# Attention, Fourier and feed-forward in one kernel: instruction order from a model clock instead of written-out counts

## The chip, the core and the metric

The kernel runs on one core of a Trainium2 chip. The metric is the device time of one execution, in microseconds. The median of three runs before the change is 1101.29 us (1101.19 to 1104.8). Engines: TensorE (PE in the rows; PEld are its weight loads), VectorE (DVE), ScalarE (ACT), GpSimd (POOL) and SyncE (SP), on whose queue all DMAs are issued. Each engine works through its own queue in order, and an instruction that waits for a semaphore holds up all that stand behind it on that engine.

## The reference

Three parts follow one another, for 4 batches of 448 rows and 768 features (12 heads of 64):

```python
scores = scale * np.matmul(q, k.transpose(0, 1, 3, 2)) - np.log(S)
attn = 1.0 / (1.0 + np.exp(-scores))
x = np.matmul(attn, v)                       # then heads side by side: (4, 448, 768)

mixed = np.real(np.fft.fft(np.fft.fft(x, axis=1), axis=2))
u = x + mixed
un = (u - mu) / np.sqrt(var + 1e-06)         # over the 768 features
y = u + np.maximum(un @ w_ch1, 0.0) @ w_ch2  # 768 -> 3072 -> 768

gate = sigmoid(causal convolution of y over 5 rows, per feature)
out = (gate * (y @ w_val)) @ w_out
```

The weights come in as float64. The kernel turns them into float32 by integer operations on VectorE, takes a power of two from the largest absolute value, and splits each matrix into a high and a low float16 half. Activations are split the same way, and three products (high x high, high x low, low x high) give the result.

## The kernel before

Features lie in six blocks of 128 partitions, rows along the free axis; `acc` holds one batch (six blocks x 448) from attention to the end.

*Attention* runs 84 steps: 24 pairs of heads (6 a batch), 7 steps for two pairs. A step is four score matmuls into `ps_s` (two buffers, L360), a sigmoid on ScalarE (L367) and, a step later, four value matmuls into `ps_m` (L380). At the end of a pair ScalarE copies one half of the result to `acc` (L386) and VectorE adds the other (L389). `ps_m` has four banks for everything else.

*Fourier* of a batch (`fourier`): the batch is folded into sums and differences of feature blocks (L399, L423) and of rows (L417 to L427), scaled by a power of two from the largest |v| (L112 to L168), split into halves `ph`, `pl` (L439), transformed over features by 40 matmuls (L468, L472), split again into `zh`, `zl` on the way out of PSUM (L268, L459), mixed over rows by 48 matmuls (L487), and added to `acc` (L494, L497). Some rows go over a small extra table (`eo`, `sp`, `e16`), which is filled by DMA.

*Norm* (`norm`): sums over the feature blocks (L569), a mean matmul (L575), centring (L588), squares (ScalarE), their sums (L591, L593), a variance matmul (L603), `rs` (L605, L606), a spread matmul (L619), scaling (L632) and halves (L626).

*Feed-forward*: 8 groups of 384 hidden features x 4 batches. `up` has 54 matmuls (L737), ScalarE and VectorE split its result (L744, L746); `down` has 54 (L760), added to `acc` by VectorE (L764). The blocks go up 0, up 1, down 0, down 1, up 2, down 2, up 3, and then up n+1, down n. A group's weights are brought in by `load_group`: chunks by DMA (L179), absolute value (L187 or L190), maximum (L198), conversion (L200, L203, L206), high half (L236, L237) and low half (L239, on GpSimd; L242, on VectorE, for the first group).

*Value and projection*, 24 blocks of 18 matmuls each (L939, L964), end the kernel.

What sets the order: the code is written out in one go, and what goes beside the main matmuls is a set of Python generators that are advanced by counts. In attention each step advances the Fourier (`fq`), the norm (`lq`) and the weights (`wq`) by fixed numbers; `ROOM`, `FOLD_AT`, `W_RATE`, `PACE`, `FFN_RATE`, `bank()` and the bare loops of `yield` in `fourier` and `norm` are such counts. Folds and sums go to GpSimd or VectorE by batch number (`E = P if b < 3 else V`). Loads of q, k and v are issued at two fixed places of each seven steps. The first weight group is loaded during attention, in chunks of 256 columns with two buffers; later groups have chunks of 384.

## Time and profile before

| | |
|---|---|
| median of the runs | 1101.29 us |
| the profiled execution | 1104.88 us |
| its span, first to last instruction | 1103.0 us |
| TensorE busy | 1042.5 us |
| VectorE busy | 709.3 us |
| ScalarE busy | 422.3 us |
| GpSimd busy | 178.6 us |
| mean granted TensorE clock | 0.981 |

The slices of the page show where it is lower. A matmul's busy time depends on the granted clock too, so a stretch can be busy all the time and yet slow; PEclk tells this. The launch lies in the 1.9 us between span and execution.

### The profile page before, as it was taken

How to read it: one execution, taken by the hardware profiler on the slowest of the kernel's cores; microseconds unless marked ns; L12 is line 12 of the kernel's file. 1: busy time of each engine (PE TensorE's matmuls, PEld its weight loads, DVE VectorE, ACT ScalarE, POOL GpSimd, SP SyncE). 2: the span in 40 equal slices, each digit the busy share in tenths (PEclk: the TensorE clock that was granted, in tenths of full speed). 3: DMA queues.
4: the chain of work that ended last, by engine and by line, in shares of the span. 5: the costliest groups of instructions: out<-in, count | busy, mean ns of one | idle time of the engine just before them, and what ended most of it. 6: DMA issues, size and time to landing. Idle time of an engine off the chain costs nothing.

```text
span 1103.0 us, 15620 instructions
## 1 busy us (share of the span) xinstructions
PE 1042.5 (95%) x6116; PEld 534.4 (48%) x6116; DVE 709.3 (64%) x1580; ACT 422.3 (38%) x630; POOL 178.6 (16%) x157
## 2 busy tenths in 40 slices
PE   9789688998979999999999999999999999999998
PEld 4244243455544455545555555555555545555554
DVE  2755678687966565776556676665666768777530
ACT  5455544544124333323333332233333274443321
POOL 0103323230002111111111101111110152000000
PEclk9899988999999999999999999999999999999999
DMA  7522223111111222333122333122233200001001
GB/s 228 171 79 83 89 67 112 33 31 30 30 29 47 68 72 72 86 86 86 43 60 73 84 86 86 48 69 71 72 86 86 59 1 1 1 26 42 34 34 67
DMA packets 34921, 72.57 MB, mean 66 GB/s; under 512 B 3956, under 2 KB 16672, under 8 KB 34848
## 3 DMA queue, kind: packets, MB, share of 16 engines
q1 hardware_dynamic: 34848, 71.58, 22.6%
q8 instruction: 48, 0.79, 0.3%
q14 instruction: 25, 0.20, 0.1%
HBM read 65.88 MB, written 5.51 MB: 65 GB/s over the span
## 4 chain that ended last, share of the span: by engine, by line
PE 73%; DVE 16%; DMA 4%; ACT 4%; issue 2%; POOL 2%; SPq 0%; ACTq 0%; DVEq 0%
PE ps_m L760 25%; PE ps_s L737 24%; PE ps_m L939 7%; PE ps_m L964 7%; PE ps_m L380 3%; DMA w<-w1d 2%; PE ps_s L360 2%; PE ps_m L468 2%; DVE acc L764 1%; PE ps_m L487 1%; DMA w<-w2d 1%; DVE wf L206 1%; DVE un L588 1%; DVE wabs L198 1%; DVE wf L203 1%
## 5 line engine op out<-in xcount | busy, mean ns | idle before, releaser
L737 PE MATMUL ps_s<-un,w1hi 128*128 128x448 f16 x1152 | 313.8, 354 | 4.9 <-DVE un L626 3.3
L760 PE MATMUL ps_m<-hh,w2hi 128*128 128x448 f16 x576 | 204.4, 355 | 5.5 <-DVE acc L764 4.1
L760 PE MATMUL ps_m<-hl,w2hi 128*128 128x448 f16 x576 | 204.2, 354 | 1.1 <-DVE hl L746 1.1
L760 PE MATMUL ps_m<-hh,w2lo 128*128 128x448 f16 x576 | 204.2, 354 | 0.0
L737 PE MATMUL ps_s<-un,w1lo 128*128 128x448 f16 x576 | 203.9, 354 | 0.0
L760 PEld LDWEIGHTS <-w2hi 128*128 128x128 f16 x1152 | 112.9, 99 | 111.0 <-issue 8.6
L737 PEld LDWEIGHTS <-w1hi 128*128 128x128 f16 x1152 | 112.9, 98 | 107.8 <-issue 4.1
L764 DVE SCALAR_TENSOR_TENSOR acc<-ps_m,rg,acc 128x448 f32<-128x448 f32 x192 | 128.5, 678 | 29.0 <-PE ps_m L760 28.7
L187 ACT ACTIVATE wabs<-w 128x384 f32<-128x384 f32 (+1 forms) x109 | 58.4, 547 | 222.4 <-DMA w<-w2d 84.1
L198 DVE TENSOR_SCALAR_CACHE_REDUCE wabs<-wabs 128x384 f32<-128x384 f32 (+1 forms) x126 | 66.8, 530 | 55.1 <-ACT wabs L187 54.3
L746 DVE SCALAR_TENSOR_TENSOR hl<-ps_s,hh 128x896 f16<-128x896 f32 x64 | 54.6, 853 | 72.0 <-ACT hh L744 72.0
L360 PE MATMUL ps_s<-q,k 64*64 64x448 f32 x672 | 84.4, 568 | 14.0 <-ACT sg L367 13.5
L367 ACT ACTIVATE sg<-ps_s,logb 128x896 f32<-128x896 f32 x84 | 82.4, 1005 | 36.6 <-PE ps_s L360 36.5
L380 PE MATMUL ps_m<-sg,v 64*64 64x448 f32 x672 | 85.5, 568 | 3.1 <-DVE vg L130 1.7
L737 PEld LDWEIGHTS <-w1lo 128*128 128x128 f16 x576 | 56.5, 98 | 56.6 <-issue 4.4
L760 PEld LDWEIGHTS <-w2lo 128*128 128x128 f16 x576 | 56.7, 98 | 54.6 <-issue 2.7
L939 PE MATMUL ps_m<-xs,wvhi 128*128 128x448 f16 x288 | 78.0, 352 | 0.0
L200 DVE TENSOR_SCALAR wf<-wabs 128x384 int32<-128x384 int32 (+1 forms) x126 | 45.1, 358 | 50.1 <-POOL w1lo L239 19.1
L744 ACT ACTIVATE hh<-ps_s 128x896 f16<-128x896 f32 x64 | 46.1, 720 | 80.0 <-PE ps_s L737 80.0
L206 DVE SCALAR_TENSOR_TENSOR wf<-w,wf 128x384 int32<-128x384 int32 (+1 forms) x126 | 71.0, 563 | 2.9
L203 DVE SCALAR_TENSOR_TENSOR wf<-w,wf 128x384 int32<-128x384 int32 (+1 forms) x126 | 68.7, 545 | 2.5
L817 DVE SCALAR_TENSOR_TENSOR gp<-acc,cw,gp 128x448 f32<-128x448 f32 x72 | 49.3, 685 | 20.3 <-ACT gp L815 18.4
(174 smaller groups left out, 1230.7 us busy)
## 6 DMA issues: line engine op xcount, KB each, us to landing
w<-w1d SPq DMA_DIRECT2D x42, 384.0 KB
w<-w2d SPq DMA_DIRECT2D x42, 384.0 KB
q<-qd SPq DMA_DIRECT2D x24, 224.0 KB
out<-o SPq DMA_DIRECT2D x24, 224.0 KB
k<-kd SPq DMA_DIRECT2D x23, 224.0 KB
w<-wvd SPq DMA_DIRECT2D x12, 384.0 KB
w<-wod SPq DMA_DIRECT2D x12, 384.0 KB
v<-vd SPq DMA_DIRECT2D x12, 256.0 KB
```

What stands on the lines that cost most here:

```text
L187: A.activation(out=wa, in_=z[:, :, 1].bitcast(F32), func=AF.Abs)
L198: V.tensor_scalar(out=a, in0=a, scalar1=LEAST, scalar2=None, op0=ALU.max, op1=ALU.max, accum_out=m[:, i:i + 1])
L203: V.scalar_tensor_tensor(out=f.bitcast(I32), in0=lo, scalar=29, in1=f.bitcast(I32), op0=ALU.logical_shift_right, op1=ALU.bitwise_or)
L206: V.scalar_tensor_tensor(out=f.bitcast(I32), in0=hi, scalar=-0x40000000, in1=f.bitcast(I32), op0=ALU.bitwise_and, op1=ALU.bitwise_or)
L360: nc.tensor.matmul(p[HALVES[c], h, :S], k[HALVES[h], ks], q[HALVES[h]], start=True, stop=True)
L367: A.activation(out=sg, in_=sc.pop(t)[:, :, :S], func=AF.Sigmoid, scale=1.0 / math.sqrt(D), bias=logb)
L380: nc.tensor.matmul(xps[at, r][HALVES[h], :S], v[HALVES[r], s, HALVES[h]], a[HALVES[r], h], start=first, stop=last)
L737: nc.tensor.matmul(p[:, i, :S], w[:, k, fs], u[:, k], start=(m == 0), stop=(m == 17))
L760: nc.tensor.matmul(p[:, :S], w[:, f, js], hh[f // 2][k][:, f % 2], start=(m == 0), stop=(m == 3 * FC - 1))
L764: V.scalar_tensor_tensor(out=acc[b][:, j, PAD:], in0=p[:, :S], scalar=rg, in1=acc[b][:, j, PAD:], op0=ALU.mult, op1=ALU.add)
L939: nc.tensor.matmul(p[:, :S], w[:, k, js], u[:, k], start=(n == 0), stop=(n == 17))
L964: nc.tensor.matmul(p[:, :S], w[:, k, js], gs[b, k][i], start=(n == 0), stop=(n == 17))
```

## The change

A model clock (`Clock`) is kept while the code is written out. Every instruction passes through `Timed`, which adds a fixed cost for its form to the model time of its engine, after the model times of its operands and free buffers. The generators no longer count steps. They yield what they need next: `on(engines, operands, cost)` or `when(condition)`. A `Board` holds them with ranks; `pump` takes the one that is ready by the model, the lowest rank first, and writes its instruction down. Where a job names two engines (folds, sums, low halves of the norm, absolute values), it goes to the one that is done first by the model. `force` writes jobs down in order of their model time until a condition holds; the main code calls it where it can't go on without (weights of a group there, a PSUM bank free).

The clock exists only while the program is written; on the chip the engines still wait for semaphores alone.

With it come: weight chunks of 384 columns in attention too, three buffers for them (two before), their absolute values on ScalarE or VectorE by the model; loads of q, k and v up to seven steps ahead; one instruction for two feature blocks in the adds after mixing and in the norm; `ps_m` as four named banks, each taken until it is read; the second Fourier batch's start bound to the first one's end; the pools for the next weight group opened when the first group is done; a smaller scratch for dynamic DMAs. Matmuls are the same in number and form.

```diff
@@ -39,49 +40,343 @@
 HALF_AT = (1, 3, 5, 6)
 AHEAD = 7
 LAG = 1
-FOLD_AT = (14, 18)
-ROOM = {1: 4, 3: 4, 5: 4}
 WARM = 9
-W_RATE = (1.85, 0.5, 1.5)
-FFN_RATE = (0.5, 2.2, 2, 1.6)
-PACE = 3
+COLS = 384
+SOON = 1.3
+IDLE = 0.6
+STEP = 1.5
+EASE = 0.9
+FOLD_BY = "DVE", "POOL"
+SUM_BY = "DVE", "POOL"
+LOW_BY = "DVE", "POOL"
+W_AT = 0
+FIRST = 7
+TABLE = 8
+ABS_BY = "ACT", "DVE"
+W_RANK = 3.5
 ABSMAX = bass.bass_isa.ReduceOp.absmax
 LEAST = 2.0 ** (896 // 8 - 127)
 
...
+    def put(self, e, cost, reads, writes, lag=0.06, shared=False, tag=None):
+        need = max([self.ready(e, *reads)] + [self.free(e, a) for a in writes])
+        start = max(self.at[e], need)
+        if shared and start < self.port[0] and self.port[1] != e:
+            cost += 0.8 * min(cost, self.port[0] - start)
+        end = start + cost
+        if shared:
+            self.port = (end, e)
...
+    def best(self, act):
+        now = self.clock.at["PE"]
+        pick = None
+        for job in self.jobs:
+            if job[3] is None:
+                if job[4] < self.turn:
+                    return job, None
+                continue
+            engines, aps, cost, go = job[3]
+            if go is not None and not go():
+                continue
+            if not engines:
+                return job, None
+            for e in engines:
+                at = self.clock.at[e]
+                t = max(at, self.clock.ready(e, *aps))
+                wait = t - max(at, now)
+                if e == "PE":
+                    ok = t <= now + 0.05
+                elif e == "ACT":
+                    ok = t + cost <= act and (wait <= 0.1 or t <= now + 0.3)
+                else:
+                    ok = t <= now + (SOON if job[0] < 4 else IDLE) and (wait <= 0.1 or t <= now + 0.3)
+                if ok:
+                    key = wait > 0.1, job[0], job[1], t + cost * (1.1 if e == "POOL" else 1)
+                    if pick is None or key < pick[0]:
+                        pick = key, job, e
+        return pick and pick[1:]
...
-    def to_f32(pl, src, dst, n, m=None):
...
+        def fetch():
+            for k in range(num):
+                yield on("SP", go=lambda: gone[0] > k - 3)
+                w = pl.tile([128, step], I64, tag="w64", bufs=3, name="w64")
+                Q.dma_start(out=w, in_=src[:, k * step:(k + 1) * step])
+                got.append(w.bitcast(I32).rearrange("p (n t) -> p n t", t=2))
+
+        def absolute():
+            for k in range(num):
+                yield when(lambda: len(got) > k and gone[0] > k - 2)
+                wa = pl.tile([128, step], F32, tag="wabs", bufs=2, name="wabs")
+                e = yield on(ABS_BY, got[k], cost=0.55)
+                if e == "ACT":
+                    A.activation(out=wa, in_=got[k][:, :, 1].bitcast(F32), func=AF.Abs)
+                else:
+                    V.tensor_scalar(out=wa.bitcast(I32), in0=got[k][:, :, 1], scalar1=0x7FFFFFFF, scalar2=None, op0=ALU.bitwise_and)
+                ready.append(wa)
+
+        board.add(rank, fetch())
...
-    def fold_part(b, t):
-        x = acc[b][:, :, PAD:]
-        if t == 0:
-            folds[b] = [fk.tile([128, 3, 4 * NE], F32, tag="pm", bufs=2, name="pm") for _ in range(2)]
-        E = P if b < 3 else V
-        for pm, op in zip(folds[b], (ALU.add, ALU.subtract)):
-            E.tensor_tensor(out=pm[:, t, :S], in0=x[:, t], in1=x[:, t + 3], op=op)
...
+                yield when(lambda: b * NT + t + 3 in stored)
+                for pm, op in zip(q, OPS):
+                    e = yield on(FOLD_BY, x[:, t], x[:, t + 3])
+                    ENG[e].tensor_tensor(out=pm[:, t, :S], in0=x[:, t], in1=x[:, t + 3], op=op)
             for k in range(2):
...
+            for o in range(2):
+                yield when(lambda: len(hls) > o)
+                yield on("PE", *hls[o], e16, go=banks(2))
+                for c in range(2):
+                    if c:
+                        yield on("PE", go=banks(1))
+                    yield from dstep(o, c, hls[o])
+            stepped.add(b)
...
-    mixed, cst, credit = {}, [], [0.0]
+    sigmoid(0)
     for t in range(NSTEP):
-        i, at = t // 7 * 2, t % 7
-        b, r = divmod(t, PER)
-        pieces[0] = ROOM.get(at, 0)
+        at_step[0] = t
+        if t == W_AT:
+            board.add(W_RANK, first_weights())
         if t + 1 < NSTEP:
             scores(t + 1)
-        sigmoid(t)
-        if t == 0:
-            amax_v(0, 0)
-        if r == 16:
-            peak_v(b, 0)
-        if r == 17:
-            pieces[0] -= 2
...
-        drain(2)
+            board.pump(ck.at["PE"] + 0.12 + EASE)
+            sigmoid(t + 1)
+        board.pump(ck.at["PE"] + STEP + EASE)
...
+    def pump():
+        tend()
+        board.pump(ck.at["PE"] + SOON + 0.8)
+
+    def force(done):
+        board.force(lambda: tend() or done())
...
@@ -733,36 +1028,33 @@
                 m = 0
                 fs = slice((f + i) * 128, (f + i + 1) * 128)
                 for k in range(NT):
+                    pump()
                     for w, u in ((w1h, un_hi[b]), (w1h, un_lo[b]), (w1l, un_hi[b])):
-                        nc.tensor.matmul(p[:, i, :S], w[:, k, fs], u[:, k], start=(m == 0), stop=(m == 17))
+                        T.matmul(p[:, i, :S], w[:, k, fs], u[:, k], start=(m == 0), stop=(m == 17))
                         m += 1
-                    if k in ((1, 3) if n < B else (2,)):
-                        yield
-                if i + 1 < nf:
...
-    nc = bacc.Bacc("TRN2", target_bir_lowering=False, num_devices=1)
+    nc = bacc.Bacc("TRN2", target_bir_lowering=False, num_devices=1, dynamic_dma_scratch_size=1024)
```

Three places in the queues, before and after. All instructions of the new kernel carry the line of `Timed` (L212), so they are told by their tiles; `acc_90`, `acc_92`, `acc_94`, `acc_96` are batches 0 to 3 before, and `acc_96`, `acc_98`, `acc_100`, `acc_102` after.

VectorE, in the norm of batch 0 (`rs`, `tt`), where the second matrix of the first weight group arrives (`w_1275` before, `w_942` and `w_945` after); before:

```order
L605 TENSOR_SCALAR rs<-ps_m 112x4
L112 TENSOR_REDUCE vm<-v 128x1
L242 SCALAR_TENSOR_TENSOR w1lo<-wf,w1s,w1hi 128x576
L612 TENSOR_SCALAR tt<-eye,rs 112x112 x4
L190 TENSOR_SCALAR wabs<-w_1275 128x256
L198 TENSOR_SCALAR wabs,wm<-wabs 128x256
L200 TENSOR_SCALAR wf<-wabs 128x256
L632 SCALAR_TENSOR_TENSOR tt<-un,ps_m 128x448 x2
L459 SCALAR_TENSOR_TENSOR zl<-ps_m,rt,zh 113x385
L203 SCALAR_TENSOR_TENSOR wf<-w_1275,wf 128x256
L632 SCALAR_TENSOR_TENSOR tt<-un,ps_m 128x448 x2
```

And after:

```order
L212 TENSOR_SCALAR wf<-wabs 128x384
L212 TENSOR_SCALAR rs<-ps_m 112x4
L212 SCALAR_TENSOR_TENSOR wf<-w_942,wf 128x384 x2
L212 TENSOR_SCALAR wabs,wm<-wabs 128x384
L212 TENSOR_SCALAR wf<-wabs 128x384
L212 TENSOR_SCALAR tt<-eye,rs 112x112 x3
L212 TENSOR_TENSOR acc_100<-acc_100,ps_m 128x448
L212 TENSOR_SCALAR tt<-eye,rs 112x112
L212 SCALAR_TENSOR_TENSOR e_117<-eo,st,e_117 12x452
L212 TENSOR_TENSOR pm<-acc_100 128x448
L212 SCALAR_TENSOR_TENSOR wf<-w_945,wf 128x384
L212 SCALAR_TENSOR_TENSOR tt<-un,ps_m 128x896
```

Before, the chunk's first instruction reads it straight after its DMA (`wabs<-w_1275`), ahead of `tt<-un` and `zl`. Now `wabs` comes from ScalarE, and `zl` of the next transform follows some rows later.

SyncE, in the first twenty microseconds (`w_…` are weight chunks, `cd` and `cst` tables of the Fourier part); before:

```order
L315 DMA q<-qd 128x448
L319 DMA k<-kd 128x448
L327 DMA v<-vd 128x384
L688 DMA cst<-csd 128x3x128
L682 DMA cd<-cdd 128x1155
L688 DMA cst<-csd 128x3x128
L682 DMA cd<-cdd 128x1155
L179 DMA w_250<-w1d 128x256
L179 DMA w_252<-w1d 128x256
L315 DMA q<-qd 128x448
L319 DMA k<-kd 128x448
L327 DMA v<-vd 128x512
```

And after:

```order
L212 DMA eye<-eyed 128x128
L212 DMA w_154<-w1d 128x384
L212 DMA w_157<-w1d 128x384
L212 DMA w_159<-w1d 128x384
L212 DMA q<-qd 128x448
L212 DMA k<-kd 128x448
L212 DMA v<-vd 128x384
L212 DMA q<-qd 128x448
L212 DMA k<-kd 128x448
L212 DMA v<-vd 128x512
L212 DMA w_261<-w1d 128x384
L212 DMA cd<-cdd 128x1155
```

The first three weight chunks moved ahead of the fourth pair's q, k and v, the tables behind the fifth's.

VectorE at the end of attention, where the feed-forward part begins (`hl` belongs to up 0, `pm`, `pl` and `eo` to Fourier, `un` and `tt` to the norm, `w2t` and `pd` to the first group's second matrix); before:

```order
L746 SCALAR_TENSOR_TENSOR hl<-ps_s,hh 128x896
L427 TENSOR_TENSOR pm<-pm 128x3x223
L417 TENSOR_TENSOR pm<-pm 128x3x113
L418 TENSOR_TENSOR pm<-pm 128x3x112
L203 SCALAR_TENSOR_TENSOR wf<-w_2232,wf 128x384
L447 TENSOR_TENSOR eo<-r_2252 12x223
L448 COPY eo<-r_2252 12x2
L447 TENSOR_TENSOR eo<-r_2252 12x223
L448 COPY eo<-r_2252 12x2
L417 TENSOR_TENSOR eo<-eo 12x2x113
L418 TENSOR_TENSOR eo<-eo 12x2x112
L439 SCALAR_TENSOR_TENSOR pl<-pm,st,ph 128x678 x2
```

And after:

```order
L212 TENSOR_TENSOR acc_100<-acc_100,ps_m 128x2x111
L212 TENSOR_TENSOR acc_100<-acc_100,ps_m 128x2x112
L212 TENSOR_TENSOR tt<-tt,acc_100 128x448
L212 TENSOR_TENSOR pm<-pm 128x3x112
L212 SCALAR_TENSOR_TENSOR pl<-pm,st,ph 128x678
L212 TENSOR_REDUCE w2t<-wm 128x1
L212 TENSOR_SCALAR pd<-eye,w2t 128x128
L212 SCALAR_TENSOR_TENSOR hl<-ps_s,hh 128x896
L212 TENSOR_TENSOR tt<-tt,acc_100 128x448 x2
L212 SCALAR_TENSOR_TENSOR pl<-pm,st,ph 128x678
L212 SCALAR_TENSOR_TENSOR hl<-ps_s,hh 128x448
L212 SCALAR_TENSOR_TENSOR un<-ps_m,acc_100 128x896 x3
```

Before, the first group's weights were finished, the second group's chunk (`w_2232`) was under way, and batch 3 was folded here. Now the end of batch 2's Fourier, its norm and the maximum of the first group's second matrix stand here, and batch 3 is folded already.

## Rows read from the trace of the kernel before

**Rows 1.** The page: TensorE's busy time, its 40 slices in tenths, granted clock
```profile
PE 1042.5 (95%) x6116; PEld 534.4 (48%) x6116; DVE 709.3 (64%) x1580; ACT 422.3 (38%) x630; POOL 178.6 (16%) x157
...
PE   9789688998979999999999999999999999999998
...
PEclk9899988999999999999999999999999999999999
```

**Rows 2.** Windows by stage: length, busy PE, PEld, DVE, ACT, POOL, clock, DMA
```profile
0.00:232.40 232.40, 196.84 (x1655) 92.10 (x1655) 145.74 (x352) 122.07 (x152) 54.54 (x48) 0.94 0.33 102
232.40:400.00 167.60, 149.17 (x782) 82.39 (x783) 122.27 (x280) 50.34 (x75) 20.83 (x19) 0.96 0.18 48
400.00:1103.00 703.00, 696.52 (x3681) 359.87 (x3678) 441.32 (x949) 249.88 (x404) 103.26 (x91) 1.00 0.21 58
```

**Rows 3.** TensorE's waits in the whole span: total us, times, longest
```profile
PE ps_s L360 <- ACT sg L367: 13.5, 11, 3.2
PE ps_m L468 <- DVE zl L459: 7.3, 2, 6.3
PE ps_m L125 <- DVE pd L119: 5.3, 3, 4.2
```

**Rows 4.** TensorE's timeline from 69 to 90 us: start, length, instructions
```profile
68.99 1.20 PE L468 MATMUL ps_m<-cd,ph 128*113 128x385 f16 x6
...
72.43 0.98 PE L380 MATMUL ps_m<-sg,v 64*64 64x448 f32 x8
...
82.50 0.41 PE L487 MATMUL ps_m<-cs,zh 113*6 113x256 f32 x2
...
85.69 0.98 PE L380 MATMUL ps_m<-sg,v 64*64 64x448 f32 x8
86.49 0.93 PE L360 MATMUL ps_s<-q,k 64*64 64x448 f32 x8
...
89.50 0.93 PE L360 MATMUL ps_s<-q,k 64*64 64x448 f32 x8
```

**Rows 5.** The chain that ended last: start, length, one block of each kind
```profile
504.78 10.21 PE ps_m L760 x54
...
963.17 3.40 PE ps_m L964 x18
```

**Rows 6.** TensorE by line: count, busy us, mean ns, idle before, releaser
```profile
L619 PE MATMUL ps_m<-tt,ones 112*128 112x112 f32 x32 | 4.8, 297 | 2.7 <-DVE tt L612 2.7
...
L125 PE MATMUL ps_m<-pd,ones_r 128*128 128x128 f32 x10 | 3.3, 345 | 7.7 <-DVE pd L119 5.3 <-DVE acc L497 2.4
```

**Rows 7.** TensorE's timeline: two waits, in brackets with what ended them
```profile
43.17 0.48 PE L125 MATMUL ps_m<-pd,ones_r 128*128 128x128 f32 x1 [4.17 <-DVE pd L119]
...
140.79 2.09 PE L468 MATMUL ps_m<-cd,ph 128*112 128x385 f16 x6 [6.25 <-DVE zl L459]
```

**Rows 8.** VectorE's timeline ahead of the second of them
```profile
138.06 0.29 DVE L190 TENSOR_SCALAR wabs<-w 128x256 int32<-128x256 int32 x1 [7.25 <-DMA w<-w2d]
...
140.13 0.61 DVE L459 SCALAR_TENSOR_TENSOR zl<-ps_m,rt,zh 113x385 fp32r<-113x385 f32 x1
```

**Rows 9.** Windows behind the first of them (columns of rows 2)
```profile
40.00:44.00 4.00, 0.83 (x5) 0.59 (x9) 3.86 (x10) 0.00 (x0) 1.79 (x2) 0.64 0.41 131
44.00:48.00 4.00, 4.00 (x24) 1.24 (x20) 3.71 (x16) 2.45 (x3) 0.00 (x0) 0.51 0.23 68
```

**Rows 10.** VectorE's waits for DMAs, 0 to 235 us
```profile
DVE vm L112 <- DMA v<-vd: 22.0, 5, 8.2
DVE wabs L190 <- DMA w<-w1d: 12.9, 5, 5.9
...
DVE wabs L190 <- DMA w<-w2d: 11.2, 2, 7.2
```

**Rows 11.** VectorE by line, 0 to 235 us: adds and folds of 448 columns
```profile
L389 DVE TENSOR_TENSOR acc<-acc,ps_m 128x448 f32<-128x448 f32 x23 | 14.2, 616 | 18.6 <-ACT acc L386 12.6 <-ACT sg L367 5.9
...
L399 DVE TENSOR_TENSOR pm<-acc 128x448 f32<-128x448 f32 x4 | 4.7, 1206 | 0.0
```

More of the change, by code (lines that the diff above doesn't have):

```diff
@@ L342, in scale_v @@
+    tabled = []
+    def scale_v(b):
+        m = keep.tile([128, NT], F32, tag="vm", bufs=2, name="vm")
+        for j in range(NT):
+            i = b * NT + j
+            yield when(lambda: i in vraw)
+            x = vraw[i][:, :4 - j % 2]
+            yield on("DVE", x)
+            amax(x, m, j)
+            maxed.add(i)
+        g = yield from peak(m, "v")
+        yield on("DVE", g)
+        e, i = pow2(g, "v")
         st = scaled(i, 2.0 ** X_EXP, "st")
@@ L431, in spill @@
         def spill(o):
-            while len(halves) <= o:
-                yield
-            yield
+            yield when(lambda: len(halves) > o and b in st_of and (b == 0 or b - 1 in stepped))
+            st, _ = st_of[b]
             pm = halves[o]
@@ L437, in spill @@
             l = fk.tile([128, 3, 2, NE], F16, tag="pl", bufs=2, name="pl")
-            yield from act(out=h, in_=pm, func=AF.Copy, scale=st)
+            yield on("ACT", pm, st, cost=0.87)
+            A.activation(out=h, in_=pm, func=AF.Copy, scale=st)
+            yield on("DVE", h)
             V.scalar_tensor_tensor(out=l, in0=pm, scalar=st, in1=h, op0=ALU.mult, op1=ALU.subtract)
             hls.append((h, l))
-            yield
+            spilt.add((b, o))
         def special():
-            for _ in range(3):
-                yield
+            yield when(lambda: all(b * NT + j in stored for j in range(NT)) and (b == 0 or b - 1 in mixed))
@@ L574, in norm @@
+        e = yield on(SUM_BY, x[:, 2], t, cost=0.6)
+        ENG[e].tensor_tensor(out=t, in0=t, in1=x[:, 2], op=ALU.add)
+        yield when(lambda: b in mixed)
+        for j in (3, 4, 5):
+            e = yield on(SUM_BY, t, x[:, j])
+            ENG[e].tensor_tensor(out=t, in0=t, in1=x[:, j], op=ALU.add)
+        yield on("PE", t, go=banks(1))
         mean = ps_m()
-        nc.tensor.matmul(mean[:, :S], ones, t, start=True, stop=True)
-        yield
-        while len(homes) <= b:
-            yield
+        T.matmul(mean[:, :S], ones, t, start=True, stop=True)
@@ new lines, in squares @@
+        def squares():
+            for k in range(3):
+                yield when(lambda: len(cen) > 2 * k + 1)
+                i = 2 * k % 4
+                if k == 2:
+                    yield when(lambda: "a" in sqs)
+                yield on("ACT", c[:, 2 * k:2 * k + 2], cost=0.95)
+                A.activation(out=tt[:, i:i + 2], in_=c[:, 2 * k:2 * k + 2], func=AF.Square)
+                sqs.append(f"s{k}")
+        board.add(1, squares())
+        for j in range(0, NT, 2):
+            yield on("DVE", mean[:, :S])
+            V.scalar_tensor_tensor(out=c[:, j:j + 2], in0=twice(mean), scalar=-1.0 / DM, in1=x[:, j:j + 2], op0=ALU.mult, op1=ALU.add)
+            cen += [j, j + 1]
@@ L597, in norm @@
+        yield when(lambda: "s2" in sqs)
+        e = yield on(SUM_BY, tt[:, 0:2])
+        ENG[e].tensor_tensor(out=tt[:, 1], in0=tt[:, 1], in1=tt[:, 0], op=ALU.add)
+        e = yield on(SUM_BY, tt[:, 1], tt[:, 3])
+        ENG[e].tensor_tensor(out=tt[:, 1], in0=tt[:, 1], in1=tt[:, 3], op=ALU.add)
         t = tt[:, 1]
-        for _ in range((2, 2, 5, 5)[b]):
-            yield
-        yield from bank()
+        yield on("PE", t, go=banks(1))
         var = ps_m()
         for i in range(4):
-            nc.tensor.matmul(var[:CK, i:i + 1], t[:, i * CK:(i + 1) * CK], ones[:, 0:1], start=True, stop=True)
+            T.matmul(var[:CK, i:i + 1], t[:, i * CK:(i + 1) * CK], ones[:, 0:1], start=True, stop=True)
@@ L634, in norm @@
+        lows = []
+        board.add(1, halves_of())
+        for j in range(0, NT, 2):
+            if j == 4:
+                yield when(lambda: lows)
+            yield on("DVE", rstd[:, :S])
+            V.scalar_tensor_tensor(out=tt[:, j % 4:j % 4 + 2], in0=c[:, j:j + 2], scalar=2.0 ** UN_EXP, in1=twice(rstd), op0=ALU.mult, op1=ALU.mult)
+            out_n.extend((j, j + 1))
+        done_m(rstd)
+        yield when(lambda: len(lows) == 3)
         normed.add(b)
     load_qk(0)
-    load_v(0, 0)
+    load_v(0)
@@ L913, in body @@
         if part is down and n // B == NG - 1:
[L914 removed]
+            board.add(2, prep_x2(b))
             if b == 0:
[L916 to L921 removed]
+                board.add(3, first_gates())
+    force(lambda: gated and not wq)
+    while late:
+        gate_ends()
     wst.close()
@@ L929, in value @@
     def value(b, j):
-        while b not in xs_of:
-            step(wq)
+        force(lambda: b in xs_of)
         xh, xl, _ = xs_of[b]
```

923 lines of the change are left out of this document (517 added, 406 removed).

## The prediction

> **What bounds the kernel now.** I read the page's busy line and its slices first: TensorE is busy 95% of the span, and its holes lie in the first 14 of the 40 slices; the granted clock dips in the same place [rows 1]. So I cut the span into three stages [rows 2]: attention up to its last value matmul at 232.4 us, the early feed-forward part up to 400 us, and the rest. TensorE lacks 35.6 us in the first stage, 18.4 us in the second and 6.5 us in the last, of which 3.6 us are the end of the last output. Busy time also holds matmuls at half clock, so I count what the same matmuls cost where they run densely at full clock:
> - an attention step (scores and values): 89.50 - 86.49 = 3.01 us for two, 1.505 us each, 84 steps: 126.4 us [rows 4].
> - Fourier: 20 matmuls take 72.43 - 68.99 = 3.44 us and 24 mixing matmuls 85.69 - 82.50 = 3.19 us [rows 4]; a batch has two of each, 13.26 us, four batches 53.0 us.
> - feed-forward: 10.21 us for 54 matmuls, 64 such blocks, 653.4 us; value and projection: 3.40 us for 18, 48 such blocks, 163.2 us [rows 5].
> - the small matmuls of the norms and the maxima: four groups, 4.3 + 3.6 + 4.8 + 3.3 = 16.0 us (the first and the last of the four stand in [rows 6]), some of it at half clock.
> - the start up to the end of the warm-up matmuls, 5.3 us, and the end, 3.6 us.
>
> The sum is 1020.9 us; the span is 1103.0 us, so 82 us are lost. The first stage holds 5.3 + 126.4 + 3 x 6.88 + 132/24 x 3.19 + 8 = 177.9 us of dense work in 232.4 us: 54.5 us lost. The last lost 6.5 - 3.6 = 2.9 us. The second has the remaining 24.7 us. Nothing below the dense sum is to be had from an order.
>
> What makes the loss: of TensorE's waits the longest in total are for the sigmoid, for the low half of a Fourier result (zl) and for a maximum (pd) [rows 3]. Two of them show the pattern. TensorE waited 6.25 us for VectorE's zl, up to 140.79 us [rows 7]; but in that time VectorE itself sat 7.25 us in front of a weight chunk whose DMA had not landed, and zl stood behind it in the queue [rows 8]. The 4.17 us before 43.17 us [rows 7] end with pd, which stands behind weight conversion in the same queue. Over the stage VectorE waited 22.0 us for values of attention and 24.1 us for weight chunks [rows 10]. After such a hole the clock is down: 0.64 and 0.51 in the 8 us from 40 us on [rows 9], the 1.2 GHz level, where the dense step takes twice its time; a wait of 4 to 6 us costs 2 to 3 us more that way.
>
> **The change, part by part.** TensorE's work is the same in number and form; only the order differs, and the floor of 1020.9 us stays.
>
> *Weights in attention.* Before, VectorE took the absolute value first, straight from the landed chunk, with two buffers and 18 chunks of 256 columns a group of weights. Now there are 12 chunks of 384, three buffers, the first three loads stand ahead of the fourth pair's q, k and v, and ScalarE takes most absolute values; a VectorE row is written down only when the model clock says that the chunk is there. In the place of the 7.25 us wait VectorE's rows now are the conversion of the chunk before and the reduction of one whose absolute value ScalarE has taken. If that holds, the 24.1 us of VectorE waiting go, and the 22.0 us for v too, since v is loaded 7 steps ahead and its maximum is written when due. On SyncE a weight load still waits for the buffer that VectorE frees, with the next pair's q, k and v behind it; those are issued 7 steps, 10.5 us, ahead of use, and that is what hides it. What is late next is VectorE's own work: it was busy 145.7 us in this stage [rows 2], and now has no more of it (fewer instructions per column, the last batch's Fourier end moved out, some sums moved in). TensorE's dense work in the stage is 177.9 - 6.88 - 36/24 x 3.19 = 166.2 us, as batch 2's Fourier comes after the last attention step. VectorE would be 88% loaded, so it still sets some waits.
>
> *Fourier and norm.* They issue when the model has their operands and free banks, batch 0 at step 41 instead of 31, batch 1 at 62. This costs nothing as long as attention steps remain to be run; that the last two batches now fall among feed-forward matmuls is covered by up 0 and up 1 (2 x 10.21 us) and by the first two batches' down blocks. Adds into two feature blocks become one instruction with twice the columns, nine a batch instead of eighteen, and the centring and scaling of the norm likewise, three for six: a small gain on VectorE, hidden by TensorE, so nothing in the sum.
>
> *Folds, sums and low halves* go to VectorE or GpSimd by the model. A row of the same shape cost VectorE 616 ns beside no GpSimd operand and 1206 ns in the worst group [rows 11]. The model charges this, so I count nothing for it in the sum, but keep 0.6 us for each of the some 30 rows that the order gives GpSimd up to the end of attention, 18 us, as the upper bound. The Trainium skill (SBUF — State Buffer, Who interferes with whom) says that the second of two such instructions blocks for the whole of the first. By that rule a collision would cost VectorE up to a whole GpSimd instruction instead of 0.6 us; the row of 1206 ns is a mean over four, so the trace bears out only the half of it.
>
> *The early feed-forward part.* Down 0 needs the second half of the first weight group. Its chain (row maximum, spread, scale, four low halves) now lies among norm 2 and Fourier 3 on VectorE; before, it was finished ahead of the stage. TensorE meets 40 Fourier matmuls and 48 mixing ones with nothing between them, so at least one evacuation is waited for there. Bounds for the stage: 0 lost, as between 69 and 90 us, where steps, transforms and mixing ran without a wait [rows 4], and the 24.7 us of now. I take 9 us, nearer to the low end, because weight group 1 no longer shares VectorE with norm 2.
>
> *Attention.* Bounds: 0 (the same stretch of rows 4) and 54.5 us. I take 15 us, about a quarter: the waits behind late DMAs go, those of a VectorE at 88% stay, each with half clock behind it.
>
> *Rest.* 2.9 us lost before; the same after.
>
> Sum: 1020.9 + 15 + 9 + 2.9 = 1047.8 us span. The profiled execution lasted 1104.88 us at a span of 1103.0, so 1049.7 us. The median of the runs is 1101.29, 3.6 us below that execution: **1046 us**.
>
> **Rivals.**
> 1. *The order comes out almost without holes.* For it: from 400 us on the kernel loses only 2.9 us in 703, and the changed order puts a job on TensorE only where its operands should be there. Against it: 88% of VectorE. With 6 us lost in the first two stages: 1020.9 + 6 + 2.9 + 1.9 - 3.6 = 1028 us.
> 2. *VectorE becomes the bound of attention by collisions with GpSimd.* With 18 us on its 145.7 and some 15 us in which it must wait for others, the stage lasts 179 us plus the half clock after some ten waits (20 us), so 33 us lost, and 12 behind it: 1020.9 + 45 + 2.9 + 1.9 - 3.6 = 1067 us. The 1206 ns group speaks for it, the 616 ns of 23 adds against it [rows 11]. It is also what the rule of the Trainium skill named above (SBUF — State Buffer, Who interferes with whom) would bring.
> 3. *The model is wrong as often as the old counts were*, so that the change only moves the holes: in-order queues then hold as before, and 1090 to 1101 us result. For it: the model's costs are fixed figures, while a wait for a chunk has no fixed length (the 24.1 us for chunks fell on a few of the 18) [rows 10]. Against it: the holes found have one cause, waiting for loads, which the new order treats.
> 4. *Slower.* TensorE's Fourier jobs are written where the model has them ready; each that it believes too early blocks all attention steps behind it in the in-order queue. There are four such places a batch (two transforms, two mixings), 16 in all. At the price of the longest hole, 6.25 us, plus 3 us of half clock, it is slower from nine places on (9 x 9.25 = 83 us); with all 16 it would be 1020.9 + 148 + 1.2 = 1170 us. Against it: the old order has the same dependence and shows one such hole of 6.25 us.
>
> **How the numbers follow.** Forecast, 1030 to 1060: 0.60. Rival 1: 0.12. Rival 2, 1060 to 1085: 0.16. Rival 3: 0.07. Rival 4: 0.05. A measurement of this kernel tells about 0.5% (5.5 us) from no change. Rivals 1 and 2 and the forecast are all faster, as is half of rival 3 and more: 0.91; same 0.04; slower 0.05. For the range I leave out the lowest part of rival 1, rivals 3 and 4 and a little of rival 2: 1026 to 1078 us.
>
> **What would show it.** Right: VectorE's waits for v and for weight chunks in attention fall from 46 us to under 10; the last value matmul ends near 181 us (166 + 15); the clock row has no more than two or three low slices; the early part has one hole between up 1 and down 0; from 400 us on nothing changes. Rival 2 would show as VectorE busy over 165 us before the last attention step and its folds at 0.9 to 1.2 us. Rival 4 would show as TensorE waiting for ph, zl or pd in holes over 5 us with attention rows behind. The forecast is wrong if TensorE's holes in attention exceed 30 us, or if the feed-forward blocks wait for weight groups, which now start to load only after the first group is done.

## The result and the profile after

| | before | after |
|---|---|---|
| median of the runs | 1101.49 us (1101.19 to 1104.8) | 1035.09 us (1032.89 to 1037.26) |
| ratio to before, 95% interval | | 0.9391 [0.9363, 0.9419] |
| profiled execution, its span | 1104.88, 1103.0 us | 1034.22, 1032.4 us |
| mean granted TensorE clock | 0.981 | 1.00 |

The change takes 66 us, 6.1%. It was forecast at 1046 us with 1026 to 1078 as the range: the direction was right, the gain 11 us larger than forecast.

The page of the changed kernel first: busy time by engine, TensorE's 40 slices, its granted clock. It answers to [rows 1].

```profile
PE 1017.3 (99%) x6116; PEld 530.8 (51%) x6116; DVE 699.3 (68%) x1486; ACT 427.2 (41%) x633; POOL 175.4 (17%) x152
...
PE   9999999989999999999999999999999999999998
...
PEclk9999999999999999999999999999999999999999
```

TensorE is busy for 25 us less, with the same 6116 matmuls: the row of clocks shows why, as no slice is at a lower one. Then the stages, cut at the new end of attention (columns of [rows 2]):

```profile
0.00:177.60 177.60, 171.77 (x1599) 85.42 (x1599) 133.24 (x277) 124.00 (x157) 39.82 (x37) 1.00 0.42 134
177.60:345.00 167.40, 163.99 (x921) 93.25 (x918) 128.22 (x270) 58.90 (x88) 36.12 (x28) 1.00 0.19 51
345.00:1032.40 687.40, 681.58 (x3602) 352.12 (x3599) 437.82 (x940) 244.27 (x388) 99.43 (x87) 1.00 0.21 59
```

TensorE lacks 5.8, 3.4 and 5.8 us, 15.1 in all; 3.7 us of the last are the end of the last output (3.6 before). Another 1.0 us is the wait ahead of the first matmul, which the dense sum holds too. With everything at full clock the rest is the loss: 15.1 - 3.7 - 1.0 = 10.4 us of idle time, where 1032.4 - 1020.9 (the dense sum of the forecast) gives 11.5 us. Before, the last value matmul ended at 232.4 us, now at 177.6.

TensorE's waits in the whole span (total us, times, longest), which answer to [rows 3]:

```profile
PE ps_m L212 <- DVE pd L212: 4.3, 4, 1.6
PE ps_m L212 <- DVE tt L212: 2.1, 1, 2.1
PE ps_m L212 <- DVE acc L212: 1.1, 1, 1.1
...
PE ps_m L212 <- POOL tt L212: 0.9, 1, 0.9
PE ps_s L212 <- ACT sg L212: 0.5, 2, 0.4
PE ps_m L212 <- POOL w2lo L212: 0.5, 1, 0.5
PE ps_m L212 <- DVE zl L212: 0.4, 1, 0.4
```

The 11 waits for the sigmoid have become two, of 0.4 us at most; zl has gone from 7.3 us to 0.4. The longest hole of the program is this one, in the norm of a batch behind attention (TensorE's timeline: start, length, instructions, idle time before):

```profile
210.95 1.15 PE L212 MATMUL ps_m<-tt,ones 112*128 112x112 f32 x8 [2.15 <-DVE tt L212]
```

VectorE's waits up to 200 us, which answer to [rows 10]:

```profile
DVE acc L212 <- ACT acc L212: 14.2, 12, 2.9
DVE acc L212 <- PE ps_m L212: 9.3, 12, 4.3
DVE vm L212 <- DMA v<-vd: 8.9, 6, 4.2
...
DVE wabs L212 <- ACT wabs L212: 2.1, 2, 1.1
```

Of 46 us in front of DMAs 8.9 are left, all of them for v, and up to 235 us none is added; no row waits for a weight chunk. The longer waits for `acc` cost TensorE one hole of 1.1 us.

### The profile page after: what moved, and what is told of

The parts are those of the page before. It is cut to its first block, busy times and chain, and to the rows that moved or that the text cites. A ratio compares the mean times of both kernels' runs of the same rounds, so it can differ in the third digit from the quotient of the medians.

```text
span 1032.4 us, 15544 instructions
## 1 busy us (share of the span) xinstructions
PE 1017.3 (99%) x6116; PEld 530.8 (51%) x6116; DVE 699.3 (68%) x1486; ACT 427.2 (41%) x633; POOL 175.4 (17%) x152
## 4 chain that ended last, share of the span: by engine, by line
PE 89%; DVE 6%; ACT 2%; POOL 1%; issue 1%; DMA 0%; ACTq 0%; SPq 0%; DVEq 0%
PE ps_m L212 56%; PE ps_s L212 33%; DVE wf L212 1%; DVE acc L212 1%; DVE gp L212 1%; DVE pm L212 1%; ACT wf L212 1%; DVE wabs L212 0%; POOL w1lo L212 0%; POOL un L212 0%; DVE tt L212 0%; DMA w<-w2d 0%; POOL w2lo L212 0%; ACT w2hi L212 0%; ACT w1hi L212 0%
## 5 line engine op out<-in xcount | busy, mean ns | idle before, releaser
L212 PE MATMUL ps_s<-un,w1hi 128*128 128x448 f16 x1152 | 312.0, 352 | 0.0
L212 PE MATMUL ps_m<-hh,w2lo 128*128 128x448 f16 x576 | 203.0, 352 | 0.5 <-POOL w2lo L212 0.5
L212 PE MATMUL ps_m<-hh,w2hi 128*128 128x448 f16 x576 | 203.0, 352 | 0.0
L212 PE MATMUL ps_s<-un,w1lo 128*128 128x448 f16 x576 | 203.0, 352 | 0.0
L212 PE MATMUL ps_m<-hl,w2hi 128*128 128x448 f16 x576 | 203.0, 352 | 0.0
L212 DVE SCALAR_TENSOR_TENSOR acc<-ps_m,rg,acc 128x448 f32<-128x448 f32 x192 | 130.8, 682 | 59.7 <-PE ps_m L212 57.6
L212 PEld LDWEIGHTS <-w2hi 128*128 128x128 f16 x1152 | 112.6, 98 | 104.6 <-issue 0.5
L212 PEld LDWEIGHTS <-w1hi 128*128 128x128 f16 x1152 | 112.3, 98 | 105.0 <-issue 1.2
L212 DVE SCALAR_TENSOR_TENSOR wf<-w,wf 128x384 int32<-128x384 int32 x240 | 135.2, 563 | 5.7
L212 DVE SCALAR_TENSOR_TENSOR hl<-ps_s,hh 128x896 f16<-128x896 f32 x64 | 54.9, 857 | 116.9 <-ACT hh L212 116.6
L212 ACT ACTIVATE wabs<-w 128x384 f32<-128x384 f32 x112 | 60.8, 554 | 165.5 <-DMA w<-w1d 48.1
L212 ACT ACTIVATE sg<-ps_s,logb 128x896 f32<-128x896 f32 x84 | 83.6, 1006 | 33.4 <-PE ps_s L212 32.5
L212 ACT ACTIVATE hh<-ps_s 128x896 f16<-128x896 f32 x64 | 46.4, 725 | 106.5 <-PE ps_s L212 106.5
L212 PE MATMUL ps_m<-sg,v 64*64 64x448 f32 x672 | 83.4, 542 | 1.1 <-DVE acc L212 1.1
L212 PEld LDWEIGHTS <-w2lo 128*128 128x128 f16 x576 | 56.4, 98 | 53.8 <-POOL w2lo L212 1.3
L212 PEld LDWEIGHTS <-w1lo 128*128 128x128 f16 x576 | 56.4, 98 | 52.6
L212 PE MATMUL ps_s<-q,k 64*64 64x448 f32 x672 | 82.7, 538 | 0.5 <-ACT sg L212 0.5
L212 DVE SCALAR_TENSOR_TENSOR gp<-acc,cw,gp 128x448 f32<-128x448 f32 x84 | 62.0, 740 | 25.7 <-ACT gp L212 23.7
L212 PE MATMUL ps_m<-xs,wvhi 128*128 128x448 f16 x288 | 78.0, 352 | 0.0
L212 DVE TENSOR_SCALAR_CACHE_REDUCE wabs<-wabs 128x384 f32<-128x384 f32 x120 | 65.4, 545 | 2.2 <-ACT wabs L212 2.1
L212 DVE TENSOR_SCALAR wf<-wabs 128x384 int32<-128x384 int32 x120 | 43.2, 360 | 13.1 <-POOL w1lo L212 7.8
L212 PE MATMUL ps_m<-xs,wvlo 128*128 128x448 f16 x144 | 50.8, 352 | 0.0
```

The costliest lines, as they stand in the source:

```text
L212: return f(*a, **k)
```

## The experiments

Theory 1: the gain comes from VectorE's queue, in which nothing stands any more that waits for a late DMA, and of that from the weight chunks above all. Theory 2: it comes from issuing each job when the model says that it can run, so that it stands and falls with the model's figures. The rows of kernels in which a line was added above `Timed` carry L214 in place of L212. Unless it says otherwise, an edit is made in the changed kernel and its time is compared with that one's 1035.1 us.

### The clock without DMA landing times

```diff
-            done = self.dma + 0.6
+            done = start
```

> The changed kernel, but its model clock takes every DMA as landed when it is issued. Theory 1 (the gain comes from knowing when a load lands, so that no VectorE instruction stands in front of a late chunk): VectorE's waits for q, k, v and weight chunks in attention come back, 20 us or more in place of 11, TensorE gets holes of 3 us and more behind them, the clock falls, and the time is 1050 us or more. Theory 2 (the gain comes from placing jobs by the engines' own times; loads are early enough anyway): within 5 us of the 1035 us of the changed kernel.

Measured: 1069.2 us (1067.9 to 1073.4), ratio to before 0.9715 [0.9682, 0.9748]. VectorE's wait for v:

```profile
DVE vm L212 <- DMA v<-vd: 45.7, 14, 5.9
```

and one of the holes in TensorE's timeline behind it:

```profile
82.53 0.47 PE L212 MATMUL ps_m<-pd,ones_r 128*128 128x128 f32 x1 [5.79 <-DVE pd L212]
```

So the landing time in the model is worth 34 us, as theory 1 of that run had it. What stands in VectorE's queue too early without it is the maximum of v, and pd behind that; for weight chunks VectorE waits only 0.5 us. The chunks stand in ScalarE's queue instead, where their absolute values are now taken, with the sigmoid behind them. TensorE's largest group of waits in this run, one wait of ScalarE for a chunk, and TensorE's hole behind it:

```profile
PE ps_s L212 <- ACT sg L212: 16.2, 8, 4.5
...
12.54 0.56 ACT L212 ACTIVATE wabs<-w 128x384 f32<-128x384 f32 x1 [4.80 <-DMA w<-w1d]
...
14.05 1.87 PE L212 MATMUL ps_s<-q,k 64*64 64x448 f32 x8 [4.52 <-ACT sg L212]
```

A table of the Fourier part does the same: ScalarE waits 4.87 us for `cst` before 53.59 us, and TensorE 3.69 us for the sigmoid before 55.06 us. So a late load costs on whichever queue it stands, and v costs more than the weight chunks.

### VectorE's costs in the model: half, a tenth less, a tenth more, one and a half

```diff
+        if e == "DVE":
+            cost *= 0.5
         return self.put(e, cost, reads, writes, shared=shared, tag=op)
```

The other three have 0.9, 1.1 and 1.5 in its place.

> The changed kernel, but its model clock counts every VectorE instruction at half its cost, so TensorE jobs are written down before VectorE is done. Theory 1 (loads): 1042 us at most, since loads stay where they are. Theory 2 (engine times): TensorE waits for VectorE's ph, zl, pd and tt in many places, some 20 us in place of 7, the clock falls behind the longest, and the time is 1055 us or more.

> Changed kernel with every VectorE cost in the model clock times 0.9. Theory 'margin': 1035 to 1055 us, a few stalls of TensorE on pd, zl or tt of 1 to 4 us each, since jobs are now written a tenth too early. Theory 'cliff': 1060 us or more, with stalls also past 400 us as in x_fast.

> Changed kernel with every VectorE cost in the model clock times 1.1 (x_fast had 0.5, x_slow 1.5). Theory 'margin': the order tolerates an error of a tenth, since most operands are ready well before their readers; 1032 to 1048 us, no stall of TensorE over 5 us. Theory 'cliff': the order is right only where the model is right; 1060 us or more, with TensorE waiting for weight pieces (w1hi, w2lo) as in x_slow.

> The changed kernel, but its model clock counts every VectorE instruction at 1.5 times its cost: TensorE jobs are written down late, never too early. If only jobs placed too early cost time (an in-order queue behind a waiting job): few waits in attention, but the Fourier jobs pile up behind its end, where forced jobs must wait: 1045 to 1060 us, well under the 1146 us of half cost. If any wrong cost is as bad as another: 1100 us or more.

| factor | median | ratio to before | clock |
|---|---|---|---|
| 0.5 | 1146.0 us (1143.8 to 1149.6) | 1.0409 [1.0374, 1.0444] | 0.967 |
| 0.9 | 1036.4 us (1035.9 to 1037.5) | 0.9410 [0.9396, 0.9424] | 0.998 |
| 1.0 | 1035.1 us | 0.9391 [0.9363, 0.9419] | 1.00 |
| 1.1 | 1054.0 us (1053.2 to 1055.6) | 0.9571 [0.9556, 0.9585] | 0.993 |
| 1.5 | 1269.9 us (1268.6 to 1270.7) | 1.1517 [1.1492, 1.1541] | 0.907 |

At 0.5 jobs are written down before their operands exist, and TensorE stands in front of VectorE's results in every stage, as theory 2 of that run had it (waits of the whole span):

```profile
PE ps_m L214 <- DVE acc L214: 34.4, 13, 4.1
PE ps_m L214 <- DVE tt L214: 17.3, 7, 3.9
PE ps_m L214 <- DVE zl L214: 9.0, 3, 4.2
```

At 1.5 it is another thing. TensorE is as busy as in the changed kernel at first (175.0 of the first 177.6 us), with less Fourier work among the attention steps: the last value matmul starts at 156.4 us. Then follow four holes of 6 to 10 us in the norms and in front of pd, 33.8 us in all, and the weights come late, and go on coming late to the end:

```profile
PE ps_s L214 <- ACT w1hi L214: 54.5, 4, 15.3
PE ps_m L214 <- ACT w2hi L214: 33.2, 8, 5.0
PE ps_m L214 <- POOL w2lo L214: 29.9, 7, 5.6
PE ps_s L214 <- POOL w1lo L214: 20.9, 4, 5.4
```

My reading, argued and not tested: a clock in which VectorE is slow has no time for the weight jobs, which come last in rank, and writes them down late, while the real VectorE is idle. In all VectorE is busy for 700.1 us, as with the right costs (699.3). That only jobs written too early cost time, the first theory of that run, is wrong: this direction is the worse of the two. At 1.1 two groups of TensorE's waits grow most: 15.0 us for pd (4.3 with the right costs), 8.67 us of them in one hole ahead of the first group's second matrix, and 4.0 us for w2lo (0.5). A tenth too little costs nothing that can be measured, and a tenth too much 19 us: neither theory of those two runs had it so lopsided.

### The third chunk buffer and ScalarE's absolute values

```diff
-                yield on("SP", go=lambda: gone[0] > k - 3)
-                w = pl.tile([128, step], I64, tag="w64", bufs=3, name="w64")
+                yield on("SP", go=lambda: gone[0] > k - 2)
+                w = pl.tile([128, step], I64, tag="w64", bufs=2, name="w64")
...
-ABS_BY = "ACT", "DVE"
+ABS_BY = "DVE",
```

The first of two runs has both edits, the second the buffers alone.

> Changed kernel with two chunk buffers in place of three and the absolute values on VectorE alone, as the kernel before had both; the model clock stays. Theory 1 (the third buffer and ScalarE are what took the chunk waits off VectorE): VectorE waits 15 us or more for w<-w1d and w<-w2d again and the time is 1045 to 1065 us. Theory 2 (it is the model's landing time, which keeps a job out of VectorE's queue until its chunk is there): waits for chunks under 8 us and 1033 to 1045 us; VectorE has some 61 us more to do, off TensorE's path.

> Changed kernel with two chunk buffers in place of three; the absolute values may again go to ScalarE or VectorE by the clock (x_w2 had two buffers and VectorE alone, and took the kernel's time before). Theory 'buffer': with two buffers a chunk's load can start only when the chunk two before it is done, so the conversion falls behind the feed-forward blocks: 1075 us or more, TensorE waiting 20 us or more for w1hi, w1lo and w2 pieces. Theory 'VectorE': it was the 61 us more work on VectorE that made the weight pieces late: 1055 us or less, under 8 us of such waits.

Measured: with both, 1102.0 us (1099.3 to 1103.3), ratio to before 0.9991 [0.9973, 1.0008]: the whole gain is gone. With the buffers alone, 1080.6 us (1079.9 to 1081.1), ratio 0.9807 [0.9774, 0.9841]. TensorE's longest waits in total of the first, and VectorE's for chunks:

```profile
PE ps_s L212 <- POOL w1lo L212: 15.1, 6, 4.6
PE ps_s L212 <- ACT w1hi L212: 10.6, 4, 3.2
PE ps_m L212 <- POOL w2lo L212: 7.4, 9, 1.1
...
PE ps_m L212 <- ACT w2hi L212: 4.6, 4, 1.1
...
DVE wabs L212 <- DMA w<-w1d: 4.6, 12, 0.6
DVE wabs L212 <- DMA w<-w2d: 2.2, 3, 0.8
```

and the same kind of waits of the second, with ScalarE's group of absolute values (count, busy us, mean ns, idle before and its releasers):

```profile
PE ps_s L212 <- ACT w1hi L212: 6.4, 2, 3.2
PE ps_m L212 <- POOL w2lo L212: 6.1, 9, 0.9
PE ps_s L212 <- POOL w1lo L212: 5.8, 3, 2.7
...
PE ps_m L212 <- ACT w2hi L212: 3.4, 3, 1.1
...
L212 ACT ACTIVATE wabs<-w 128x384 f32<-128x384 f32 x94 | 50.9, 548 | 180.3 <-DMA w<-w1d 78.6 <-DMA w<-w2d 57.5 <-DVE wf L212 17.2
```

Both theories of the first run are wrong in the point that matters: VectorE waits only 6.8 us for chunks (theory 2), and yet nothing is left of the gain, since it is the feed-forward blocks that now wait for weight pieces, 37.7 us in four such groups, and TensorE is busy for 27 us more at a clock of 0.974. In the second, TensorE waits 21.7 us for such pieces, and the clock is 0.976; theory 'buffer' holds. ScalarE waits 136 us for chunks there, against 96 in the changed kernel. A chunk lands 3.2 us after its issue (median of that run), and with two buffers it can be issued only when the chunk two before it is through. VectorE's own work on the absolute values is then worth 21 us more (its busy time goes from 706.2 to 740.0 us, 34 us more; the expectation said 61, which is ScalarE's busy time for them). Why the old order, with two buffers, loses only 2.9 us behind 400 us was not tried.

### The old counts with the third buffer, and with v earlier

In the kernel before: three chunk buffers, three loads ahead, and four empty turns before the first group's first use of a chunk (the smaller scratch for dynamic DMAs makes the room). Buffers and loads ahead hold for all weight groups, the empty turns for the first alone.

```diff
-            w = pl.tile([128, step], I64, tag="w64", bufs=2, name="w64")
+            w = pl.tile([128, step], I64, tag="w64", bufs=3, name="w64")
...
-        ahead = [load(s) for s in range(0, min(n, 2 * step), step)]
+        ahead = [load(s) for s in range(0, min(n, 3 * step), step)]
+        for _ in range(4 if step == WCOLS else 0):
+            yield
...
```

The second run adds a fifth buffer for v and loads v one pair earlier.

```diff
-            if nxt + 1 < NPAIR:
-                load_v(*divmod(nxt + 1, NT))
+            if nxt + 2 < NPAIR:
+                load_v(*divmod(nxt + 2, NT))
...
```

> The kernel before, with one thing changed in its first weight group: three chunk buffers in place of two, three loads issued ahead, and four empty turns between the first loads of a matrix and its first VectorE instruction. Theory 1 (loads): VectorE's waits for weight chunks fall from 24 us to under 8, the 6.25 us hole before zl goes, and the time falls by 10 to 20 us, to 1081 to 1091 us. Theory 2: less than 5 us.

> The kernel before with the gap and third buffer for weight chunks (1079 us), and besides each pair's v loaded one pair earlier into a fifth buffer. Theory 1 (late loads in front of VectorE): its waits for v in attention fall from 22 us to under 8, and the time by 5 to 15 us more, to 1064 to 1074 us. If those waits were harmless: 1079 us.

Measured: 1079.0 us (1078.0 to 1079.7), ratio 0.9797 [0.9765, 0.9829], and 1074.2 us (1071.5 to 1076.3), ratio 0.9739 [0.9709, 0.9769]. VectorE's waits for DMAs in the first:

```profile
DVE vm L112 <- DMA v<-vd: 21.6, 6, 6.8
...
DVE wabs L192 <- DMA w<-w1d: 3.9, 1, 3.9
```

and in the second:

```profile
DVE vm L112 <- DMA v<-vd: 7.4, 3, 4.7
DVE wabs L192 <- DMA w<-w1d: 3.8, 1, 3.8
```

The chunk waits of [rows 10] go from 24.1 to 3.9 us, and the run is 22.5 us shorter. Most of that is in attention: of the 26.2 us between the two profiled spans 20.5 lie ahead of the last value matmul, which now ends at 211.9 us; what the third buffer does for the later groups was not separated. The waits for v go from 21.6 to 7.4 us, and the run is 5 us shorter again. So 27 of the 66 us are to be had without a clock. With the same two kinds of wait nearly gone, the old order still ends 39 us behind the new one: theory 1 explains two fifths.

The trace of the second run shows where the 39 us lie. TensorE is idle for 43.1 us (15.1 in the changed kernel), 21.9 of them up to the last value matmul, and busy for 12.2 us longer at a clock of 0.995. Its longest waits in total are for the sigmoid, 11.9 us. In two of them, before 52.36 and 168.20 us, no load is late: ScalarE's queue has `ph` of the Fourier part ahead of the sigmoid, and `ph` waits 2.75 and 2.64 us for VectorE's `pm`, while VectorE works without a wait for a DMA. There it is the order that costs.

### Which engine takes folds, sums and low halves

```diff
-FOLD_BY = "DVE", "POOL"
-SUM_BY = "DVE", "POOL"
-LOW_BY = "DVE", "POOL"
+FOLD_BY = "POOL",
+SUM_BY = "POOL",
+LOW_BY = "POOL",
```

The second run has `"DVE",` three times.

> The changed kernel, but folds, sums and low halves of the norm all go to GpSimd, without a choice. If the choice of the engine is worth little (my view: these chains have slack behind attention steps): within 5 us of 1035 us. If the choice is a main part of the gain: 1050 us or more, with TensorE waiting for GpSimd's tt, un or pm in place of 1.4 us now.

> The changed kernel, but folds, sums and low halves of the norm all go to VectorE. VectorE gets some 30 instructions of 0.6 us more in attention (about 20 us on 133), GpSimd 37 us less and no collisions. If GpSimd's share of that work is needed: 1040 to 1050 us, with VectorE near 155 us busy in the stage. If collisions eat what it saves: 1035 us or less.

Measured: GpSimd alone 1053.7 us (1050.7 to 1056.2), ratio 0.9567 [0.9535, 0.9599]; VectorE alone 1050.1 us (1049.1 to 1051.1), ratio 0.9524 [0.9503, 0.9545]. The long holes of the two in TensorE's timeline, GpSimd alone:

```profile
188.52 0.29 PE L212 MATMUL ps_m<-cs,zl 112*6 112x256 f32 x1 [4.23 <-DVE zl L212]
...
269.30 2.05 PE L212 MATMUL ps_m<-tt,ones 112*128 112x112 f32 x8 [11.11 <-DVE tt L212]
```

VectorE alone:

```profile
209.74 1.62 PE L212 MATMUL ps_m<-ones,tt 128*112 128x1 f32 x8 [6.86 <-DVE tt L212]
...
236.03 1.83 PE L212 MATMUL ps_m<-tt,ones 128*128 128x448 f32 x2 [6.05 <-DVE tt L212]
```

Attention has none of these holes. If VectorE takes all, it was expected to be busy for some 155 us in attention; it is busy for 128.8 of the first 177.6 us. The choice is worth 15 to 19 us, nearly all of it in the stage of the norms behind attention (177.6 to 345 us), where TensorE lacks 16.4 and 18.8 us in place of 3.4, at clocks of 0.95 and 0.94. VectorE is busy there for 134.7 of 167.4 us if it takes all (128.2 with the choice). With GpSimd alone the longest hole has this behind it:

```profile
268.97 0.84 DVE L212 TENSOR_SCALAR tt<-eye,rs 112x112 f32<-112x112 f32 x4 [13.44 <-POOL rs L212]
```

On GpSimd a maximum over the partitions of the weights (PARTITION_ALL_REDUCE, 260.76 us) stands ahead of `rs`, with 6.43 us of idle time before it and 6.71 us after it for which the profile names no cause. So that hole is not shown to come from the adds. Their price is higher on GpSimd all the same:

```profile
L212 POOL TENSOR_TENSOR pm<-acc 128x448 f32<-128x448 f32 x14 | 19.4, 1392 | 95.1 <-DVE acc L212 95.1
```

That is a fold of the changed kernel; VectorE does the same fold in 618 ns (mean of 24) in the run where GpSimd has no folds, and in 698 ns (mean of 10) in the changed kernel.

### TensorE's side jobs 0.4 us later

```diff
-                    ok = t <= now + 0.05
+                    ok = t <= now + 0.05 and self.clock.ready(e, *aps) <= now - 0.4
```

> The changed kernel, but a TensorE job beside attention or the feed-forward blocks is written down only when its operands have been ready for 0.4 us by the model, in place of at once. If the remaining waits for pd, tt and zl (9 us in all) are the model being a little early: they halve, 1030 to 1033 us. If the later place costs as much: 1035 us, no difference.

Measured: 1041.2 us (1040.0 to 1042.8), ratio 0.9444 [0.9423, 0.9466], some 6 us more than without, which neither theory had (1030 to 1033 us, or no difference). TensorE waits less for pd (3.2 us in place of 4.3) and has new holes elsewhere, the longest of 3.30 us in front of `acc` and this one, here with the clock behind it (timeline, then windows of 4 us, columns of [rows 2]):

```profile
128.81 1.01 PE L212 MATMUL ps_m<-sg,v 64*64 64x448 f32 x2 [2.51 <-DVE zl L212]
...
124.00:128.00 4.00, 2.29 (x13) 1.02 (x11) 3.90 (x6) 2.94 (x5) 2.71 (x2) 1.00 0.38 91
128.00:132.00 4.00, 3.19 (x20) 1.23 (x24) 4.00 (x9) 0.00 (x0) 2.50 (x2) 0.59 0.46 164
```

None of these kernels is faster than the changed one; the one with factor 0.9 is level with it.

## Why the prediction came out as it did

**The floor.** 1020.9 us held: with every slice at full clock, the span less the idle time above comes to 1022.0 us.

**Attention, 15 us forecast.** The dense work was put at 166.2 us up to the last value matmul. Half of batch 2's first transform (3.4 us, [rows 4]) now lies before it too, so 169.6; it ended at 177.6, and at most 8 us are lost, 4.8 of them as holes. The signs named came: VectorE's waits for DMAs fell from 46 to 8.9 us (under 10 was forecast), the end is at 177.6 (forecast 181), and there is no slice at a low clock (two or three were forecast). What failed is the step "those of a VectorE at 88% stay, each with half clock behind it". VectorE is busy 133.2 of 177.6 us, 75%, since 12.5 us of its former 145.7 lie elsewhere or have gone; and no hole of this stage is longer than 1.16 us. Its granted clock is 1.00, so there was no half clock to pay for. Set against the dense work, as the forecast did it, VectorE's load is 79% (133.2 of 169.6).

**Early feed-forward part, 9 us forecast.** About 3 (3.4 us lacking between 177.6 and 345 us). The hole was expected between up 1 and down 0, at an evacuation of Fourier; the one that came is in the norm (`tt`, 2.15 us).

**Rest, 2.9 us forecast.** 5.8 - 3.7 = 2.1 us: as forecast. All the terms that were off were off the same way, towards too much loss.

**Folds, sums and low halves.** Nothing was counted for them, and 18 us was the bound for collisions. The folds pay 80 ns each on VectorE (698 against 618 ns), and the next sums more: `pm` of 128x669 takes 1280 ns (mean of 8) against 848 where GpSimd has none of this work. Together with the two smaller sums that is about 6 us, inside the bound. Of the rule that the second of two such instructions blocks for the whole of the first (the Trainium skill, SBUF — State Buffer, Who interferes with whom) the forecast said that the trace bears out only the half, since the group of 1206 ns is a mean over four. Read one by one, the four fit it whole: two take 0.62 us, one takes 1.24 us behind the start of a GpSimd instruction, and the last takes 2.34 us, beside a GpSimd instruction that by the profile began 0.02 us ahead of it (both rows before the change):

```profile
230.88 1.89 POOL L626 TENSOR_TENSOR un<-tt,un 128x896 f16<-128x896 f32 x1 [0.39 <-ACT un L268]
230.90 2.34 DVE L399 TENSOR_TENSOR pm<-acc 128x448 f32<-128x448 f32 x1
```

In the changed kernel two of the ten folds on VectorE meet a running GpSimd instruction in this way (1.19 us from 38.91 us, 0.82 us from 89.25 us); where VectorE's began first, as at 30.05 and 43.76 us, it took 0.62 us and GpSimd's 1.58 in place of 1.14. One pair does not fit: at 77.88 us GpSimd began first, and its fold took 1.99 us, VectorE's 0.62. So the price of a single collision was read too low; in the sum over the rows it stayed inside the bound. What I missed is that the choice itself is a gain: 15 to 19 us, in the early feed-forward part.

**The third buffer.** The forecast named it among the parts and put its worth into the waits for chunks in attention. It is worth 45 us under the clock (1080.6 to 1035.1), most of it by weight pieces that the feed-forward blocks would otherwise wait for: 21.7 us as waits, and TensorE is busy for 23.6 us longer at the lower clock. That the blocks might wait was named as what would make the forecast wrong; it does not happen, and the buffer with ScalarE's share is why.

**From span to median.** 3.6 us were taken off because the profiled execution before was above its median. The one after is 0.9 us below its own. So the span was 15.4 us too high, and the median only 10.9: 4.5 us of the agreement are chance.

**The rivals.** Rival 1 (almost without holes, 1028 us) was as near as the forecast: it is 7 us below the result, the forecast 11 above. Rival 2 is out (VectorE 133 us in attention, folds at 0.70 us). Rival 3 is out for the change as made (with two buffers and ScalarE left out the time is the old one, but by late weights and not by moved holes). Rival 4 did not come, but it was real: at half of VectorE's costs the same code takes 1146 us, by jobs written too early, while at nine tenths it loses nothing.

**What the 66 us are made of** can't be given as a sum of parts. From the old side, late DMAs off VectorE's queue bring 27 us. From the new side, taking away a single thing costs 15 (choice of engine), 34 (landing times) or 45 us (third buffer), together more than the gain: the parts overlap and need one another. Several parts of the change were not tried alone: the chunks of 384 columns in attention, the loads of q and k seven steps ahead, the joined adds, and ScalarE's share of the absolute values with three buffers.

## What to carry to other kernels

An order from a model clock is as good as its costs, and not alike on both sides: here a tenth too cheap on VectorE was free, a tenth too dear cost 19 us, and half as much again made the kernel 15% slower than with hand-set counts. So the costs are to be measured from a trace, and here an error downwards of a tenth was the cheaper one; at one and a half the weights, last in rank, came late. Before building a planner, look at what stands at the head of the queue that the busiest engine waits for: a load issued earlier and a third buffer gave 27 of 66 us with the old counts. And a buffer's worth is to be asked again under the new order: the third one was worth 45 us under the new one, and at most 22.5 (with loads further ahead) under the old.
